# Two matrix products issued among the attention's last steps, and one PSUM pool for both stages

## The chip, the cores and the metric

The kernel runs on one core of one Trainium2 chip. The metric is the device time of one execution in microseconds (us); lower is better. The engines are named as the profile names them: PE (TensorE, matmuls; PEld is its weight load), DVE (VectorE), ACT (ScalarE), POOL (GpSimd), SP (SyncE, which issues the DMAs here). Each engine runs its own instructions in the order in which the program wrote them and waits on semaphores for the others.

## The reference

```python
def _attn_ref(q, k, v, w1, b1, w2):              # q, k, v: 4 x 8 heads x 576 x 64
    scores = scale * np.matmul(q, k.transpose(0, 1, 3, 2))
    x = (psi_rel / psi_i)[..., None]             # log1p of distances over log1p of the row
    bias = np.maximum(x @ w1 + b1, 0.0) @ w2     # one bias per head
    scores = scores + bias.transpose(2, 0, 1)[None]
    attn = softmax(scores)
    return np.matmul(attn, v)

def _moe_ref(x, w1, w2, w3, w_out):              # x: 2304 x 512, w1..w3: 512 x 768
    h = np.maximum(np.maximum(x @ w1, x @ w2), x @ w3)
    return h @ w_out
```

The attention's output, heads side by side, is the x of the second part. Everything is fp32 at the boundary.

## The kernel before

**Three stages.** First the bias of the attention is built and parked in HBM. Then the attention runs in 72 steps (`NSTEP`), one per tile of query rows, and four more steps without new scores (`LAG` is 4). Last comes the matrix stage: x times the three weight matrices with a maximum, then times w_out. The program is written in its final order (`manual_schedule`): what stands earlier in the code is earlier on its engine.

**An attention step.** Step n computes scores on PE (`front`), adds the bias and takes the maximum on DVE (`shift`), exponentials on ACT, normalization on POOL (`norm`), and, four steps late, `flip`: PE transposes the attention rows into the PSUM tiles `tp` (two) and `lp`, and ACT and DVE copy them to the tile `et`. Then `products` takes a few pieces of attention times values from a queue; their sum lies in the PSUM tile `pv`, which `split_x` (L427, DVE) copies into the blocks of x. In steps 72 to 75 no scores are made: each is a flip (transposes of 64 rows at a time, L366) and two or three pieces of `pv` (128 rows by 64 columns, L407). The last sum, `pvlast`, lies in a place of the tag `t`. Its last four matmuls read the tile `vl1`, the left-over rows of the values.

**The matrix stage** multiplies 2 x 2 block matrices by a scheme of seven products p1 to p7 instead of eight. x has the blocks b11, b12, b21, b22 and sums of them, t1 to t4; the weights too. Each operand is split into a high and a low part in a format that PE multiplies in one pass: `high` is a cast on ACT (L583), `low` a subtraction on DVE or POOL (L560, the line of the helper `arith`). A product is 2 x 3 matmuls (L670 high by high, L671 with the low part of x, L672 with the low part of the weights), six in all, of 128x128 by 384 columns. A group is the seven products of one third x of the tokens with one weight set s; the first groups are (s, x) = (0, 0), (1, 0), (0, 1), (1, 1). The order on PE is p5, p6, p2, p7, p1 of the next group, p4, p3.

**Three PSUM places per group.** p1, p5 and p2 each take a new place from `bank`. p6, p7 and p4 are added onto p1's place, p3 onto p5's. So each of them can start only when the one before it has been read out: p6 after ACT copied p1 (m1, L691), p7 after ACT copied p6 (u2, L699), p4 after ACT copied p7 (u3, L706), and p3 after DVE added u3 to p5 (in the first group the DVE instruction `ht<-p,u` whose inputs are p5 and u3; "p5's add" below).

**Work between the products.** Ahead of each product there is a slot in which listed jobs run (`at(n, k, ...)`: group n, slot k). Slot (0, 0) stands ahead of p5 of the first group. The jobs prepare the second third of x (`b1`) and weight set 1: `raise_w(1, 0)` and `raise_w(1, 1)` are its casts on ACT (768 and 1024 columns, into the tile `wh1`), `lower_w` the subtractions on DVE (`wl`).

**The end of the attention.** After step 75 the rest of `pv` and `pvlast` is issued, then t2's low part and the sum t4 on DVE, the cast of t4 on ACT, its low part on DVE, and `split_x` for `pvlast`. Only then is the attention's PSUM pool released and a new one opened with eight places of one tag, `p`.

**Places in SBUF.** The pools of the matrix stage have `reuse_waits="tile"`: the first instruction that writes a new tile waits for every user of each earlier tile that lies on any of the new one's bytes. In the program's address map of one partition, `wh1` lies at bytes 128160 to 135328. The attention's `bias3` (125344 to 129952), `bias4` (129952 to 134560), `vl0` (134560 to 135072) and `vl1` (135072 to 135584) lay there before. The tile of m1 (126624 to 128160) lies on `bias3` alone.

Lines that the text names beside these: L311 `shift`, L339 POOL's normalization, L477 and L481 the copies of the transposes, L747 and L749 `raise_w`.

Of the kernel before, what the change touches and what calls it, by code (L numbers as in the profile page):

```python
# [9 lines left out]
F32 = mybir.dt.float32  # L10
# [4 lines left out]
PSUM = bass.MemoryType.PSUM  # L15
# [4 lines left out]
def kernel(  # L20
# [12 lines left out]
    nc = tc.nc  # L33
# [13 lines left out]
    psums = []  # L47
    dram = ctx.enter_context(tc.tile_pool(name="dram", bufs=1, space=DRAM))

    def ps_s(name, tag="s"):  # L50
        return psums[-1].tile([128, 2, 512], F32, tag=tag, bufs=2, name=name)

    def early(name):
        return psums[-1].tile([128, 1024], F32, tag="bp", bufs=4, name=name)

    def bank(name):
        return psums[-1].tile([128, 512], F32, tag="p", bufs=8, name=name)

    def ps_t(name):
        return psums[-1].tile([128, 512], F32, tag="t", bufs=2, name=name)  # L60
# [3 lines left out]
    TW = 384  # L64
# [5 lines left out]
    xs = {}  # L70
# [142 lines left out]
    NSTEP = len(sched)  # L213
# [8 lines left out]
    class Attention:  # L222
# [125 lines left out]
        def flip(self, n):  # L348
            pair, y = fronts[n]
            which, t = step_of(pair, y)  # L350
            pool, e2 = self.pool, self.st.pop(n)["e"]
            if y == MIX:
                self.group(2 * pair + 1, 1)
                parts = [(2 * pair, GW, 0, LEFT), (2 * pair + 1, GW, LEFT, LEFT)]
            else:
                un = 2 * pair + which
                if y in (0, 2, 7):
                    self.group(un, int(y == 2))
                parts = [(un, 128 * (t % 2), 0, 128)]
            lp = psums[-1].tile([128, 128], F32, tag="l", bufs=1, name=f"lp{pair}_{y}")  # L360
            tps = [ps_t(f"tp{pair}_{y}_{r}") for r in range(2)]
            blocks = [(2 * c + h, S * h + 128 * c + LEFT * h) for h in range(2) for c in range(NTQ)]

            def turn(r, to, k0):
                p = slice(64 * r, 64 * r + 64)
                return nc.tensor.transpose(to, e2[p, k0:k0 + 128], ident[p, p])  # L366

            a = turn(0, lp[:, 0:64], LB)
            for i, (o, k0) in enumerate(blocks):
                turn(1, tps[1][:, 64 * o:64 * o + 64], k0)  # L370
                turn(0, tps[0][:, 64 * o:64 * o + 64], k0)
            b = nc.tensor.nop()
            tc.add_manual_dep(b.ins, a.ins.name, mybir.DependencyInfo(
                mybir.DependencyClass.Sync, mybir.DependencyReason.DATA), reason="two row tiles write one bank")
            turn(1, lp[:, 64:128], LB)
            out = []
            for r in range(2):
                src = tps[r].rearrange("p (c h q) -> p c h q", c=NTQ, h=2)
                un, c0 = parts[r if y == MIX else 0][0:2]
                c0 += 0 if y == MIX else 64 * r  # L380
                out.append([(self.et[un][0][:, :, :, c0:c0 + 64], src)])
            out.append([(self.et[un][1][:, c0:c0 + w], lp[:, r:r + w]) for un, c0, r, w in parts])
            return out

        def queue_pv(self, un, g, ea, el):
            hp, b = units[un]
            u = self.data[un]
            made = []
            x = GW if (hp + g) % 2 else 0
            ranges = [(x, GW)] + ([(2 * GW, LEFT)] if g else [])  # L390
            w0 = sum(w for _, w in ranges)
            last = un == len(units) - 1 and not g

            def pair(c):
                def run():
                    if c == 0:
                        self.split_x()

                        if last:
                            made.append(ps_t("pvlast")[:, 0:w0])  # L400
                        else:
                            made.append(psums[-1].tile([128, w0], F32, tag="pv", bufs=1, name=f"pv{un}_{g}"))
                    pv = made[0]
                    for h in range(2):
                        p = slice(64 * h, 64 * h + 64)
                        w, x = (u["vt"][:, c, h], ea[:, c, h]) if c < NTQ else (u["vl"][:, h], el)
                        nc.tensor.matmul(pv[p], lhsT=w, rhs=x, start=(c == 0), stop=(c == NTQ))  # L407
                    if c == NTQ:
                        slot = ((1, 0), (2, 3))[hp // 2][b // (B // 2)]
                        o = 0  # L410
                        for c0, w in ranges:
                            col = (b % (B // 2)) * S + c0
                            for x in range(NX):
                                lo, hi = max(col, TW * x), min(col + w, TW * x + TW)
                                if lo < hi:
                                    self.done.append((pv[:, o + lo - col:o + hi - col],
                                                      raws[x][slot][:, hp % 2, lo - TW * x:hi - TW * x]))
                            o += w
                        return True
                return run  # L420

            self.wait = True
            self.pvq.extend(pair(c) for c in range(NTQ + 1))
# [7 lines left out]
        def step(self, n, more=(), behind=()):  # L431
            m, f = n - BATCH, n - LAG
            if n < NSTEP:
                pair, y = fronts[n]
                which, t = step_of(pair, y)
                un = 2 * pair + which
# [29 lines left out]
            ends = bool(done) or n % NS == 7  # L466

            def empty():
                tp0, tp1, left = self.flip(f)
                if lead and n < NSTEP:  # L470
                    for h in range(2):
                        self.shift(n, h)
                    if split:
                        self.expo(n, 0)
                shared = FILL + 2 <= n < NS + 2
                for x in tp0 + ([] if shared else left):
                    nc.scalar.copy(*x)  # L477
                if turned:
                    products()
                for x in tp1 + (left if shared else []):  # L480
                    nc.vector.tensor_copy(*x)  # L481
# [45 lines left out]
            if n < NSTEP:  # L527
                pair, y = fronts[n]
                k = n - (NS * pair + (3 if pair else 5))
# [94 lines left out]
    wf = {}  # L624
# [21 lines left out]
    def sum_w(raw, sr):  # L646
        g = nc.gpsimd
        for o, a, b, op in ((part(sr, 0), part(raw, 0), part(raw, 2), ALU.add),
# [6 lines left out]
    PRODUCTS = dict(p1=(0, "b11"), p2=(2, "b21"), p3=(6, "b22"), p4=(1, "t4"), p5=(3, "t1"), p6=(4, "t2"),  # L655
                    p7=(5, "t3"))

    def moe(pool, wpool, x0, xa, xb, raw, sr):
        ht = pool.tile([128, NX, 4, TW], F32, name="ht", bufs=1)
        hd = h_d.rearrange("(f p) (t n) -> p f t n", p=128, t=2)  # L660
        xb_ = [x0] + [Blocks(x, xa, xb) for x in range(1, NX)]
        v, g = nc.vector, nc.gpsimd

        def terms(o, w, xn, r, first, last, again=False):
            hi, lo = w
            h, l = xn
            for j in range(2):
                c = slice(r + 128 * j, r + 128 * j + 128)
                on = dict(skip_group_check=again)
                nc.tensor.matmul(o, lhsT=hi[:, c], rhs=h[:, j], start=first and j == 0, stop=False, **on)  # L670
                nc.tensor.matmul(o, lhsT=hi[:, c], rhs=l[:, j], start=False, stop=False, **on)  # L671
                nc.tensor.matmul(o, lhsT=lo[:, c], rhs=h[:, j], start=False, stop=last and j == 1, **on)  # L672

        def group(s, x):

# [2 lines left out]
            o = {}  # L678
# [2 lines left out]
                return pool.tile([128, TW], F32, tag=name, bufs=bufs, name=f"{name}{s}_{x}")  # L681

            def made(p, on=None):
                o[p] = o[on] if on else bank(f"{p}_{s}_{x}")[:, 0:TW]
                w, n = PRODUCTS[p]
                terms(o[p], wf[s], xs[x][n], 256 * w, not on, True, bool(on))
                return o[p]
# [69 lines left out]
        b0, b1, b2 = xb_  # L757
        F = lambda f, *a: (lambda: f(*a))
        for k, what in {
                (0, 0): (F(b1.sum, "t1"), F(raise_w, 1, 0), F(b1.high, "b11"), F(lower_w, 1, 0, v, 3)),  # L760
                (0, 2): (F(raise_w, 1, 1),),
                (0, 3): (F(lower_w, 1, 3, v, 4),),
                (0, 4): (F(b1.high, "t1", "b21"),),
                (0, 5): (F(b1.low, "t1"), F(b1.sum, "t3")),
# [38 lines left out]
        for s in range(2, NSET):  # L803
            n = 3 * s - 3
# [70 lines left out]
        for x in range(len(order)):  # L875
            n = 4 + x
# [46 lines left out]
        n = 3 * NSET - 3  # L923
# [76 lines left out]
        n = 3 * NSET  # L1000
        for m in range(NP):
            at(*((n - 8, 0) if m == 0 else (n - 1, 0) if m == 1 else (n + m - 2, 0)), F(load_h, m))
            w = n + m - 1
# [109 lines left out]
    with tc.manual_schedule():  # L1113
# [3 lines left out]
        at = Attention(apool)  # L1117
        n = 0
# [198 lines left out]
            w.rest()  # L1317
        x0.low("t2")
        x0.sum("t4")
        x0.high("t4")  # L1320
        x0.low("t4")
        at.split_x()
        apool.release()
        psums.pop().release()
        psums.append(ctx.enter_context(tc.tile_pool(name="psum_m", bufs=1, space=PSUM, reuse_waits="tile")))
        xb = ctx.enter_context(tc.tile_pool(name="xb", bufs=1, side="right", reuse_waits="tile"))
        with tc.tile_pool(name="moe_p", bufs=1, reuse_waits="tile") as mp:
            moe(mp, wpool, x0, xa, xb, last["raw"], last["got"]["sr"])


_OUT = ((2304, 512), "float32")
# [43 lines left out]
```

## Time and profile before

| | before |
|---|---|
| median of 3 runs | 530.75 us (529.96 to 531.67) |
| the profiled execution | 530.31 us |
| its span in the profile | 528.4 us |
| PE busy | 518.6 us, 98% of the span |
| DVE, ACT, POOL busy | 437.5, 356.9, 261.4 us |
| attention's last flip / first matmul of the matrix stage | 257.20 / 261.30 us |

The profile is one execution. All its times count from the start of its span. The time outside the span is 1.9 us. A row of the timeline gives the start, the time taken, the engine, the line, the operation, what it writes and reads, and how many such instructions are merged; in brackets how long the engine was idle before and who released it. Matmuls overlap each other, so the distance from start to start tells the pace, not the time taken. The same holds in part for DVE and ACT, where one instruction begins about 0.1 us before the last has ended.

### The profile page before, as it was taken

The numbers are of one execution on the slowest core, as the hardware profiler recorded it, in microseconds if no ns is written. First come the engines' busy times: TensorE is split into PE (matmuls) and PEld (weight loads), VectorE is DVE, ScalarE is ACT, GpSimd is POOL, SyncE is SP. The second block draws the span as 40 slices with busy tenths as digits, with TensorE's granted clock in tenths as the row PEclk, the third lists the DMA queues.
The fourth block names the chain that finished last, engine by engine and source line by source line (L and its number), as shares of the span: only waits on it lengthen the run. The fifth ranks groups of instructions, "written<-read, shape, count | busy, mean of one in ns | idle before, by whom it ended". The sixth has DMA issues, their size and how long they took to land.

```text
span 528.4 us, 13630 instructions
## 1 busy us (share of the span) xinstructions
PE 518.6 (98%) x5167; PEld 433.5 (82%) x5167; DVE 437.5 (83%) x932; ACT 356.9 (68%) x802; POOL 261.4 (49%) x290
## 2 busy tenths in 40 slices
PE   8998999999999999999999999999999999999997
PEld 4464667676767676767699999999999999999997
DVE  7998979898989898988899888648887556898883
ACT  8997989999989999988666443442434425465552
POOL 0003877677878798887600055466637455300000
PEclk9999999999999999999999999999999999999999
DMA  5995988534675184214010115342247270856642
GB/s 161 277 334 164 326 280 224 178 96 122 198 244 153 25 235 126 71 24 143 3 40 2 40 56 188 137 145 95 78 167 253 81 243 7 258 166 194 187 154 81
DMA packets 73474, 78.66 MB, mean 149 GB/s; under 512 B 23168, under 2 KB 54528, under 8 KB 73408
## 3 DMA queue, kind: packets, MB, share of 16 engines
q1 hardware_dynamic: 73264, 77.49, 46.9%
q8 instruction: 41, 0.67, 0.5%
q10 hardware_dynamic: 144, 0.29, 0.2%
q14 instruction: 25, 0.20, 0.1%
HBM read 49.56 MB, written 27.94 MB: 147 GB/s over the span
## 4 chain that ended last, share of the span: by engine, by line
PE 95%; DVE 2%; issue 1%; DMA 1%; ACT 0%; DVEq 0%; ACTq 0%
PE pv L407 16%; PE p L670 13%; PE p L671 12%; PE p L672 12%; PE s L301 12%; PE bp L140 8%; PE tp L366 6%; PE p_o L1041 4%; PE p_o L1040 4%; PE p_o L1039 4%; PE s L291 2%; PE lp L366 2%; DVE sn L311 1%; DMA sm<-in_small_dram 1%; PE pvlast L407 0%
## 5 line engine op out<-in xcount | busy, mean ns | idle before, releaser
L339 POOL TENSOR_SCALAR e<-e,rc 128x576 f32<-128x576 f32 x144 | 111.2, 788 | 31.3 <-DVE rc L335 25.8
L311 DVE CUSTOM_DVE_ANT_0 sn<-s,bias 128x576 f32<-128x576 f32 x144 | 103.2, 754 | 23.2 <-PE lp L366 12.4
L325 ACT ACTIVATE e<-sn,nm 128x576 f32<-128x576 f32 x144 | 111.4, 780 | 5.6 <-DVE nm L311 5.4
L407 PE MATMUL pv<-et,vt 128*64 128x320 f32 (+1 forms) x496 | 74.0, 419 | 0.1
L366 PE MATMUL tp<-ident,e 64*128 64x64 f32 x1152 | 53.2, 224 | 0.5 <-ACT et L477 0.3
L481 DVE COPY et<-tp 128x512 f32<-128x512 f32 x72 | 49.3, 685 | 3.0 <-PE tp L366 2.9
L301 PE MATMUL s<-kh,qh 64*128 64x288 f32 x240 | 48.2, 343 | 2.8 <-DVE nm L311 2.7
L477 ACT COPY et<-tp 128x512 f32<-128x512 f32 x72 | 41.8, 580 | 12.7 <-PE lp L366 11.9
L366 PEld LDWEIGHTS tp<-ident,e 64*128 64x128 f32 x1152 | 47.4, 139 | 0.9 <-ACT et L477 0.4
L301 PEld LDWEIGHTS s<-kh,qh 64*128 64x128 f32 x240 | 28.1, 185 | 23.2 <-DVE nm L311 9.2
L560 POOL TENSOR_TENSOR ws<-wr 128x256 f32<-128x256 f32 x16 | 12.4, 773 | 69.0 <-ACT u L699 49.6
L407 PEld LDWEIGHTS pv<-et,vt 128*64 128x64 f32 x496 | 30.2, 136 | 17.8 <-issue 1.6
L140 PE MATMUL bp<-hid,w2s 128*32 128x79 f32 (+51 forms) x640 | 40.3, 391 | 1.1 <-DVE hid L117 0.8
L699 ACT COPY u<-p 128x384 f32<-128x384 f32 x27 | 13.0, 480 | 41.6 <-PE p L672 41.5
L301 PE MATMUL s<-kl,qh 64*128 64x288 f32 x240 | 41.0, 296 | 0.0
L301 PE MATMUL s<-kh,ql 64*128 64x288 f32 x240 | 39.9, 291 | 0.0
L117 DVE TENSOR_SCALAR hid<-wls,bp 128x528 f32<-128x528 f32 (+17 forms) x108 | 39.0, 446 | 0.0
L140 PEld LDWEIGHTS bp<-hid,w2s 128*32 128x32 f32 x640 | 21.3, 109 | 20.7 <-issue 13.5
L706 ACT COPY u<-p 128x384 f32<-128x384 f32 x27 | 12.9, 479 | 36.9 <-PE p L672 36.7
L366 PE MATMUL lp<-ident,e 64*128 64x64 f32 x144 | 33.1, 230 | 1.1 <-ACT et L477 0.4
L560 DVE TENSOR_TENSOR q<-p,u 128x384 f32<-128x384 f32 x36 | 20.0, 555 | 14.4 <-ACT u L706 12.0
L366 PEld LDWEIGHTS lp<-ident,e 64*128 64x128 f32 x144 | 19.8, 137 | 13.6 <-issue 8.1
(209 smaller groups left out, 1625.9 us busy)
## 6 DMA issues: line engine op xcount, KB each, us to landing
bias_d<-bs SPq DMA_DIRECT2D x36, 295.5 KB, 5.4
w<-in_moe_w_dram SPq DMA_DIRECT2D x36, 256.0 KB, 3.1
bias<-bias_d SPq DMA_DIRECT2D x15, 576.0 KB, 5.2
h_d<-ht SPq DMA_DIRECT2D x18, 384.0 KB, 3.2
hin<-h_d SPq DMA_DIRECT2D x16, 384.0 KB, 4.5
qr<-in_qd_dram SPq DMA_DIRECT2D x16, 288.0 KB, 4.7
kr<-in_kd_dram SPq DMA_DIRECT2D x16, 288.0 KB, 5.1
vt<-in_v_dram SPq DMA_DIRECT2D x32, 128.0 KB, 2.8
```

Of the source, the lines that this page charges most:

```text
L140: nc.tensor.matmul(bp[32 * c:32 * c + 32, o:o + w], lhsT=w2s, rhs=src, start=True, stop=True)
L301: nc.tensor.matmul(ss[h][:, x, 0:HALF], lhsT=u[q][p, 128 * t:128 * t + 128], rhs=u[k][p, cols], start=(j == 0), stop=(j == len(terms) - 1))
L311: nc.vector.tensor_tensor_reduce(out=sn.rearrange("p (a b) -> p a b", a=2), in0=st["s"][h][:, :, 0:HALF], in1=bt.rearrange("p (a b) -> p a ...
L325: nc.scalar.activation(st["e"][:, S * h:S * h + S], sn, ACTF.Exp, scale=-1.0, bias=nm, accum_out=self.sm[:, x:x + 1])
L339: nc.gpsimd.tensor_scalar(out=e, in0=e, scalar1=self.rc[:, x:x + 1], scalar2=1.0, op0=ALU.mult, op1=ALU.mult)
L366: return nc.tensor.transpose(to, e2[p, k0:k0 + 128], ident[p, p])
L407: nc.tensor.matmul(pv[p], lhsT=w, rhs=x, start=(c == 0), stop=(c == NTQ))
L477: nc.scalar.copy(*x)
L481: nc.vector.tensor_copy(*x)
L670: nc.tensor.matmul(o, lhsT=hi[:, c], rhs=h[:, j], start=first and j == 0, stop=False, **on)
L671: nc.tensor.matmul(o, lhsT=hi[:, c], rhs=l[:, j], start=False, stop=False, **on)
L672: nc.tensor.matmul(o, lhsT=lo[:, c], rhs=h[:, j], start=False, stop=last and j == 1, **on)
```

## The change

The matrix stage takes its PSUM places from the attention's tags instead of a pool of its own: six in turn, two of tag `s`, two of `t`, one `l`, one `pv`. The attention's pool therefore stays open to the end. p1 and p5 of group (0, 0) are issued inside the attention: p1 in step 73 ahead of the flip, p5 in step 74 behind the flip. `terms` moves out of `moe` for that. The group later takes them from `ahead`. The cast and the low part of t4 and the `split_x` of `pvlast` move from the end of the attention into slot (0, 0), behind both casts of weight set 1 on ACT and behind its first subtraction on DVE; `raise_w(1, 1)` moves there from slot (0, 2), and t1 and b11 of the second third stand behind them.

```diff
+    ring = []
+
     def bank(name):
-        return psums[-1].tile([128, 512], F32, tag="p", bufs=8, name=name)
+        if not ring:
+            ring.extend("ssttlp")
+        k = ring.pop(0)
+        if k == "s":
+            return ps_s(name)[:, 0]
+        return ps_t(name) if k == "t" else one_bank(name, "l" if k == "l" else "pv")
+
+    def one_bank(name, tag):
+        return psums[-1].tile([128, 512], F32, tag=tag, bufs=1, name=name)
...
             def empty():
+                if n == NSTEP + 1:
+                    begin("p1")
                 tp0, tp1, left = self.flip(f)
+                if n == NSTEP + 2:
+                    begin("p5")
...
-    def moe(pool, wpool, x0, xa, xb, raw, sr):
+    def terms(o, w, xn, r, first, last, again=False):
...
+    ahead = {}
+
+    def begin(p):
+        w, n = PRODUCTS[p]
+        ahead[p] = bank(f"{p}_0_0")[:, 0:TW]
+        terms(ahead[p], wf[0], xs[0][n], 256 * w, True, True)
+
+    def moe(pool, wpool, x0, xa, xb, raw, sr, split_x):
...
             def made(p, on=None):
+                if (s, x) == (0, 0) and p in ahead:
+                    o[p] = ahead[p]
+                    return o[p]
...
-                (0, 0): (F(b1.sum, "t1"), F(raise_w, 1, 0), F(b1.high, "b11"), F(lower_w, 1, 0, v, 3)),
-                (0, 2): (F(raise_w, 1, 1),),
+                (0, 0): (F(raise_w, 1, 0), F(raise_w, 1, 1), F(b0.high, "t4"), F(lower_w, 1, 0, v, 3), F(b0.low, "t4"),
+                         split_x, F(b1.sum, "t1"), F(b1.high, "b11")),
                 (0, 3): (F(lower_w, 1, 3, v, 4),),
...
         x0.low("t2")
         x0.sum("t4")
-        x0.high("t4")
-        x0.low("t4")
-        at.split_x()
         apool.release()
-        psums.pop().release()
-        psums.append(ctx.enter_context(tc.tile_pool(name="psum_m", bufs=1, space=PSUM, reuse_waits="tile")))
```

The tiles `lp` and `pv` are also taken as whole places of 512 columns (`one_bank`) and cut to size.

## Rows read from the trace of the kernel before

**Rows 1.** The page: busy time, share of the span and instructions of each engine.
```profile
PE 518.6 (98%) x5167; PEld 433.5 (82%) x5167; DVE 437.5 (83%) x932; ACT 356.9 (68%) x802; POOL 261.4 (49%) x290
```

**Rows 2.** Chain that ended last, around the last attention sum: start, us, what.
```profile
259.20 2.17 PE pvlast L407 x20
```

**Rows 3.** Stretches: busy time and instructions of each engine, PE clock, DMA share, GB/s.
```profile
249.00:252.00 3.00, 2.40 (x30) 1.37 (x28) 2.58 (x7) 2.97 (x10) 2.00 (x4) 1.00 0.61 224
...
268.70:276.00 7.30, 7.30 (x44) 7.30 (x44) 7.27 (x11) 4.46 (x9) 0.00 (x0) 1.00 0.21 68
276.00:283.30 7.30, 7.30 (x43) 7.14 (x41) 7.27 (x11) 4.27 (x7) 0.00 (x0) 1.00 0.00 0
```

**Rows 4.** Timeline of PE, 253 to 264 us.
```profile
253.22 0.22 PE L366 MATMUL lp<-ident,e 64*128 64x64 f32 x1
253.37 0.76 PE L407 MATMUL pv<-et,vt 128*64 128x320 f32 x4
...
255.15 0.22 PE L366 MATMUL lp<-ident,e 64*128 64x64 f32 x1
255.44 1.84 PE L407 MATMUL pv<-et,vt 128*64 128x320 f32 x12
...
259.04 1.90 PE L407 MATMUL pvlast<-et,vt 128*64 128x256 f32 x16
260.76 0.61 PE L407 MATMUL pvlast<-et,vl 128*64 128x256 f32 x4
261.30 0.44 PE L670 MATMUL p<-b11h,wh 128*128 128x384 f32 x1
261.58 0.34 PE L671 MATMUL p<-b11l,wh 128*128 128x384 f32 x1
...
263.49 0.33 PE L670 MATMUL p<-t2h,wh 128*128 128x384 f32 x1
```

**Rows 5.** The low weights: the last instruction before 261 us that writes them.
```profile
L560 DVE TENSOR_TENSOR wl<-ws,wh x1: 967/967/967, 239.1 to 239.1; 128x512 fp32r<-128x512 f32 x1
```

**Rows 6.** Timeline of DVE, 259 to 283 us.
```profile
259.82 0.95 DVE L560 TENSOR_TENSOR t2l<-t,t2h 128x768 fp32r<-128x768 f32 x1
260.68 0.95 DVE L560 TENSOR_TENSOR t<-xb,t 128x768 f32<-128x768 f32 x1
262.66 0.96 DVE L560 TENSOR_TENSOR t4l<-t,t4h 128x768 fp32r<-128x768 f32 x1 [1.03 <-ACT t4h L583]
...
264.74 0.95 DVE L560 TENSOR_TENSOR wl<-wr,wh 128x768 fp32r<-128x768 f32 x1
265.77 0.56 DVE L560 TENSOR_TENSOR ht<-p,m 128x384 f32<-128x384 f32 x1
...
267.38 0.55 DVE L560 TENSOR_TENSOR ht<-p,u 128x384 f32<-128x384 f32 x1
268.06 0.96 DVE L560 TENSOR_TENSOR t1l<-t,t1h 128x768 fp32r<-128x768 f32 x1
...
282.80 0.55 DVE L560 TENSOR_TENSOR ht<-p,u 128x384 f32<-128x384 f32 x1
```

**Rows 7.** Timeline of ACT, 261 to 266 us.
```profile
261.72 0.83 ACT L583 CAST t4h<-t 128x768 fp32r<-128x768 f32 x1 [2.96 <-DVE t L560]
...
263.02 0.84 ACT L747 CAST wh<-wr 128x768 fp32r<-128x768 f32 x1
263.76 0.84 ACT L583 CAST b11h<-xb 128x768 fp32r<-128x768 f32 x1
264.73 0.48 ACT L699 COPY u<-p 128x384 f32<-128x384 f32 x1
265.11 1.05 ACT L749 CAST wh<-ws 128x1024 fp32r<-128x1024 f32 x1
```

**Rows 8.** Timeline of PE at p3 of the third group.
```profile
283.13 0.34 PE L672 MATMUL p<-t4h,wl 128*128 128x384 f32 x1
283.40 0.45 PE L670 MATMUL p<-b22h,wh 128*128 128x384 f32 x1
```

More of the change, by code (lines that the diff above doesn't have):

```diff
@@ L359, in flip @@
                 parts = [(un, 128 * (t % 2), 0, 128)]
-            lp = psums[-1].tile([128, 128], F32, tag="l", bufs=1, name=f"lp{pair}_{y}")
+            lp = one_bank(f"lp{pair}_{y}", "l")[:, 0:128]
             tps = [ps_t(f"tp{pair}_{y}_{r}") for r in range(2)]
@@ L401, in run @@
                         else:
-                            made.append(psums[-1].tile([128, w0], F32, tag="pv", bufs=1, name=f"pv{un}_{g}"))
+                            made.append(one_bank(f"pv{un}_{g}", "pv")[:, 0:w0])
                     pv = made[0]
@@ L656 @@
                     p7=(5, "t3"))
-    def moe(pool, wpool, x0, xa, xb, raw, sr):
+    def terms(o, w, xn, r, first, last, again=False):
+        hi, lo = w
+        h, l = xn
+        for j in range(2):
+            c = slice(r + 128 * j, r + 128 * j + 128)
+            on = dict(skip_group_check=again)
+            nc.tensor.matmul(o, lhsT=hi[:, c], rhs=h[:, j], start=first and j == 0, stop=False, **on)
+            nc.tensor.matmul(o, lhsT=hi[:, c], rhs=l[:, j], start=False, stop=False, **on)
+            nc.tensor.matmul(o, lhsT=lo[:, c], rhs=h[:, j], start=False, stop=last and j == 1, **on)
+    ahead = {}
[4 more added lines that the diff above has]
+    def moe(pool, wpool, x0, xa, xb, raw, sr, split_x):
         ht = pool.tile([128, NX, 4, TW], F32, name="ht", bufs=1)
@@ L662, in moe @@
         v, g = nc.vector, nc.gpsimd
[L664 to L672, printed above, removed]
         def group(s, x):
@@ L1319 @@
         x0.sum("t4")
-        x0.high("t4")
-        x0.low("t4")
-        at.split_x()
         apool.release()
-        psums.pop().release()
-        psums.append(ctx.enter_context(tc.tile_pool(name="psum_m", bufs=1, space=PSUM, reuse_waits="tile")))
         xb = ctx.enter_context(tc.tile_pool(name="xb", bufs=1, side="right", reuse_waits="tile"))
         with tc.tile_pool(name="moe_p", bufs=1, reuse_waits="tile") as mp:
-            moe(mp, wpool, x0, xa, xb, last["raw"], last["got"]["sr"])
+            moe(mp, wpool, x0, xa, xb, last["raw"], last["got"]["sr"], at.split_x)
+        psums.pop().release()
 _OUT = ((2304, 512), "float32")
```

## The prediction

> **What bounds the kernel now.** I read the page's busy shares first: PE works 98% of the span [rows 1]. Then the chain that ended last: around the border of the two stages it runs on PE alone, through the pieces of `pv`, `pvlast` (2.17 us) and then the products without a break [rows 2]. Then the stretches: PE is full from 268.70 to 283.30 us, and DVE nearly so, 7.27 of 7.30 us twice [rows 3]. DVE therefore has no room to catch up there. The timeline shows that it already sets PE's start in one place: p3 of the third group begins 0.27 us after the matmul before it instead of the usual 0.17, and p5's add on DVE ended at 282.80 + 0.55 = 283.35, 0.05 us before p3's 283.40 [rows 6, 8]. So the kernel is bound by PE, and around the border by whatever makes PE late; work that only moves along PE gains nothing. The change can gain where PE waits now, and lose where ACT or DVE come later than PE needs them.
>
> **What PE gains and loses in the last steps.** I call the start of the first product 261.30 us S. p1 and p5 take S to 263.49, 2.19 us; 0.11 of it is the longer distance behind the first matmul (0.28 against 0.17), so the twelve matmuls are 2.08 [rows 4]. They don't vanish: they are issued earlier, and everything behind them in steps 73 to 75 moves back by the same 2.08.
>
> Each of the two adds one border between unlike shapes on PE. Such borders are in the rows: the last two pairs of `pvlast` take 0.54 to the first product, where pairs follow each other at 1.72 / 8 = 0.215, so 0.11 is lost, and another 0.11 behind the first matmul [rows 4]. No row has a product followed by a transpose or by `pv`. From below such a border costs 0, from above 0.22. p1 stands between `pv` and transposes, where there was a border already; its own start is the measured one, so I take 0.22 for it. p5 stands between transposes and `pv`; I take 0.11, the middle. p5 also fills a wait: in step 74 `pv` starts 0.29 us behind the last transpose, in step 73 0.15 [rows 4], so 0.14 goes. Together PE comes to the matrix stage 0.22 + 0.11 - 0.14 = 0.19, say 0.2 us later in net; the ends are -0.14 (borders free) and 0.44 (both dear, the wait not filled). PE's larger idle time, 0.6 of the 3 us from 249 to 252 [rows 3], lies in step 72, ahead of p1, and stays. The operands are there: the low weights were complete at 239.12 + 0.97 = 240.09 [rows 5].
>
> The Trainium skill, in "TensorEngine Tiling (Array Packing)", section Tiling Modes, says that a change of the tiling mode drains TensorE, which speaks against the change: both products stand between modes. By it both borders are dear and the term would be 0.22 + 0.22 - 0.14 = 0.30, and the sum below 0.1 more. The border that rows 4 show agrees with it; those that the change makes, no row shows.
>
> **What ACT does next.** p6 now is the first product behind `pvlast`; call its start P. It takes the place that p1 had, so P = S + 2.08 + 0.2 = 263.6. ACT has copied m1 long before, since p1 was done in step 73, and goes to the job list: both casts of weight set 1, then t4's cast, then b11's of the second third, then u2.
>
> The first of these casts now waits. It is the first write to `wh1`, which shares its last 256 bytes with `vl1`, and `vl1` is read by the last four matmuls of `pvlast` [rows 4]. A new tile's first write waits for all users of what lay on its bytes, so the cast starts when `pvlast` has ended, although it doesn't itself write those bytes. Before, this wait couldn't be seen: the cast stood behind m1 and began at 263.02, 1.72 us behind the first product [rows 7]. `pvlast`'s last matmul ends about when the first product starts, so I set the cast at P + 0.1.
>
> From there ACT works back to back, with distances from start to start of [rows 7]: 0.74 for a 768-wide cast (263.02 to 263.76), 0.95 for the 1024-wide one (1.05 less the usual overlap of 0.1). So: first cast P + 0.11, second P + 0.85, t4 P + 1.80, b11 P + 2.54, u2 P + 3.28, ended P + 3.76. p7 may start at P + 3.80. Undisturbed it would start two products and one border behind P, at P + 0.11 + 2 x 1.04 = P + 2.19. **PE stalls 1.61 us ahead of p7.** Before, u2 ended at 264.73 + 0.48 = 265.21 and p7 was due at 263.49 + 2 x 1.04 = 265.57: no stall, because the 1024-wide cast stood behind u2 and t4's ahead of the first product.
>
> If the wait on `vl1` weren't there, ACT would wait for t4's sum instead. That sum follows `pv`'s last copy and t2's low part on DVE, all behind PE, so it keeps its distance: 260.68 + 0.95 = S + 0.33, now P + 0.33. Then t4's cast starts at P + 0.42 and u2 ends at P + 2.38: a stall of 0.23. These are the two ends of this term; I take the upper, because the overlap of the bytes is a fact of the program.
>
> **What DVE does next.** Before, it idled 1.03 us ahead of t4's low part [rows 6]; the new order puts weight set 1 there. But t4's cast ends at P + 2.63, so the low part starts at P + 2.7. From that one's start to p5's add were 267.38 - 262.66 = 4.72 us, of which 265.77 - 264.74 = 1.03 were weight set 1's, now done ahead [rows 6]. So p5's add starts at P + 6.39 and ends at P + 6.94; p3 may start at P + 6.99. PE reaches p3 three products behind p7, at P + 6.92. So PE is late by 0.07 more here. The `split_x` for `pvlast` lies in this block at about P + 3.6 to P + 4.0; the next p1 takes `pvlast`'s place at P + 4.84, so it costs nothing.
>
> p3 was at 263.49 + 5 x 1.04 = 268.69 = S + 7.39. It is now at P + 6.99 = S + 9.27: 1.9 us late. DVE is later than that: its add was at S + 6.08 and is at S + 2.28 + 6.39 = S + 8.67, 2.6 late. It wins back the idle ahead of `t1l`, 268.06 against 267.93 and the overlap of 0.08, 0.21 in all, and then nothing to 282.80, where it is full [rows 3, 6]. So p3 of the third group, which follows p5's add by 0.05 already [rows 8], comes **2.38 us late**. Behind it PE is as busy as before and has no slack to give this back.
>
> **Parts at nothing.** Six places in turn instead of eight: p1's place is next written two groups on, five products (5.2 us) behind p4, p5's seven products behind p3, while p5's add, for example, ended at 267.93, 1.3 us after p7 [rows 6]. If readers came over 5 us late it would cost their excess. The attention's own readers of the places of `s` end before: the last scores are read in step 71, two steps ahead of p1. One pool less to open and release costs nothing, since no wait stood at 261.30 but the border. No DMA moves on SP's queue, and POOL has no new work; its last two low parts are needed by p2 and p3 only.
>
> **The sum.** 0.2 in the last steps, 1.61 + 0.07 at p7 and p3 of the first group, and 0.5 that DVE's lag adds by the third group: 2.4 us. The profiled execution (span 528.4, its own time 530.31) would take 532.7. The median of the runs is 0.44 above that execution; with it I predict 533.1.
>
> **Rivals.**
>
> First, ACT doesn't wait for `pvlast`. Then the stall at p7 is 0.23, p3 starts at P + 5.6 (three products behind P + 2.42, and p5's add ends at P + 1.34 + 3.69 + 0.55 = P + 5.58), DVE's add is 2.28 + 5.03 - 6.08 = 1.23 late, less 0.21 is 1.0. 530.75 + 1.0 = 531.8. For it: nothing in the trace shows the wait. Against it: the bytes.
>
> Second, on the other side: ACT and DVE keep up. DVE no longer idles its 1.03 us, and weight set 1 is prepared while PE is still at `pvlast`. It decides at whether both casts are done before t4's sum, at P + 0.33, that is, started by P - 1.4, and t4's sum comes that early too. Then p3's late start goes (0.10 in the third group [rows 8], as much again for the slow matmul behind it, and, as an estimate, the same in the fourth: 0.4), and the wait of 0.14: 530.75 - 0.5 = 530.2. For it: DVE's idle time is real, and ACT has nothing else to do ahead of P. Against it: t4's sum stands behind `pv`'s last copy, which stands behind the two moved products.
>
> Third, the change doesn't do what it says: a product waits in step 73 or 74 for its place or its operands, and the flip behind it waits too. Rows 5 speak against it; it would cost what it waits, and at some tenths be no different from the first rival, 531.5.
>
> **How the numbers follow.** The forecast has 0.62, with a range of its own from 532.5 to 533.7 (its unknown borders, -0.14 to 0.44, and the scatter of a median); the first rival 0.20, the second 0.13, the third 0.05. The range is 531.0 to 534.0: it takes in the first and the third rival and leaves out the second and the tails. About 0.3% is what a measurement of this kernel can tell from no change, 1.6 us, so the bounds are 529.2 and 532.3. Slower by more: nine tenths of the forecast and a little of the first rival, 0.60. Within: the rest of these, the third rival and most of the second, 0.33. Faster: 0.07.
>
> **What would show it.** In the changed kernel's timeline: six products' matmuls ahead of the transposes of step 73 and six behind those of step 74, with `pv` 0.15 to 0.4 us behind; `wh` on ACT starting within 0.2 us of `pvlast`'s end, and ACT idle ahead of it; u2 about 3.3 us behind p6's start; a gap of 1.6 us on PE ahead of p7, put down to ACT; DVE's idle ahead of t4's low part moved to the cast of t4; no further wait on PE except short ones at p3. The prediction is wrong if `wh` starts before `pvlast` ends, if PE's sum of gaps from 249 to 291 us grows by less than a microsecond, or if PE later wins the time back.

## The result, and the profile after

The changed kernel takes 532.55 us (median of five runs, 532.34 to 535.16); the kernel before took 529.96 in the same comparison (five runs, 529.63 to 531.67). The ratio is 1.0057, 95% interval 1.0037 to 1.0077: slower by about 3 us. The profiled execution took 532.68 us with a span of 530.8, against 530.31 and 528.4.

The page of the changed kernel, its line of busy times, which answers to [rows 1]: as many instructions on each engine, PE 2.9 us longer busy.

```profile
PE 521.5 (98%) x5167; PEld 434.2 (82%) x5167; DVE 436.5 (82%) x932; ACT 357.3 (67%) x802; POOL 261.0 (49%) x290
```

The chain that ended last, of the changed kernel, from `pvlast` on (start, us, what), answers to [rows 2]. It no longer stays on PE: behind `pvlast` it goes through five operations of ACT and comes back at p7.

```profile
260.69 2.18 PE pvlast L417 x20
262.89 0.27 ACT wh L771
263.17 0.47 issue
263.63 0.52 ACT wh L773
264.23 0.36 issue
264.58 0.83 ACT t4h L597
265.41 0.73 ACT b11h L597
266.15 0.38 ACT u L723
266.53 0.04 issue
266.57 0.44 PE p L678
```

The waits of PE in the changed kernel (engine, line, what it waited for: total us, times, longest) have one entry that no wait of before answers to:

```profile
PE p L678 <- ACT u L723: 1.4, 1, 1.4
```

The timeline of PE in the changed kernel (start, time taken, instruction, how often; in brackets the idle time and its releaser), in the stretch of [rows 4], shifted by the two products:

```profile
251.77 0.44 PE L678 MATMUL p<-b11h,wh 128*128 128x384 f32 x1
...
252.75 0.34 PE L680 MATMUL p<-b11h,wl 128*128 128x384 f32 x1
253.02 0.27 PE L376 MATMUL lp<-ident,e 64*128 64x64 f32 x1
...
255.50 0.22 PE L376 MATMUL lp<-ident,e 64*128 64x64 f32 x1
255.65 0.45 PE L678 MATMUL p<-t1h,wh 128*128 128x384 f32 x1
255.93 0.34 PE L679 MATMUL p<-t1l,wh 128*128 128x384 f32 x1
...
256.65 0.34 PE L680 MATMUL p<-t1h,wl 128*128 128x384 f32 x1
256.92 1.84 PE L417 MATMUL pv<-et,vt 128*64 128x320 f32 x12
...
262.78 0.44 PE L678 MATMUL p<-t2h,wh 128*128 128x384 f32 x1
...
264.79 0.34 PE L680 MATMUL p<-b21h,wl 128*128 128x384 f32 x1
266.57 0.44 PE L678 MATMUL p<-t3h,wh 128*128 128x384 f32 x1 [1.44 <-ACT u L723]
...
284.99 0.44 PE L678 MATMUL p<-b22h,wh 128*128 128x384 f32 x1
```

p1 and p5 stand where the change puts them, and p6 of the first group (262.78) comes straight behind `pvlast`. Between p2's last matmul (264.79) and p7's first (266.57) lie 1.78 us instead of 0.17.

ACT of the changed kernel, 262 to 267 us, answers to [rows 7]. It waits for `pvlast`, and then works back to back until u2.

```profile
262.89 0.83 ACT L771 CAST wh<-wr 128x768 fp32r<-128x768 f32 x1 [2.26 <-PE pvlast L417]
263.63 1.05 ACT L773 CAST wh<-ws 128x1024 fp32r<-128x1024 f32 x1
264.58 0.83 ACT L597 CAST t4h<-t 128x768 fp32r<-128x768 f32 x1
265.32 0.83 ACT L597 CAST b11h<-xb 128x768 fp32r<-128x768 f32 x1
266.05 0.47 ACT L723 COPY u<-p 128x384 f32<-128x384 f32 x1
```

DVE of the changed kernel, 262 to 285 us, answers to [rows 6]; the last row is p5's add of the third group, which ends 0.05 us ahead of p3:

```profile
262.17 0.95 DVE L574 TENSOR_TENSOR t<-xb,t 128x768 f32<-128x768 f32 x1
263.76 0.96 DVE L574 TENSOR_TENSOR wl<-wr,wh 128x768 fp32r<-128x768 f32 x1 [0.64 <-ACT wh L771]
265.52 0.96 DVE L574 TENSOR_TENSOR t4l<-t,t4h 128x768 fp32r<-128x768 f32 x1 [0.80 <-ACT t4h L597]
...
269.19 0.55 DVE L574 TENSOR_TENSOR ht<-p,u 128x384 f32<-128x384 f32 x1
...
284.39 0.55 DVE L574 TENSOR_TENSOR ht<-p,u 128x384 f32<-128x384 f32 x1
```

**Two stretches make up the difference.** I measure the border from the start of step 71's `pv` group with the left-over values (248.72 before, 247.83 after; "the anchor" below), ahead of everything that the change moves, to the start of p3 of the third group. Before that was 283.40 - 248.72 = 34.68 us, after 284.99 - 247.83 = 37.16: 2.48 longer. From there to the output stage both profiles agree to 0.01 us, so nothing is given back. The second stretch I had not looked for: the output stage, from its first to its last matmul, took 68.18 before and 68.97 after, 0.79 more. The rest of the difference of the two spans, -0.89, lies ahead of the border (the anchor itself moves by that much), and a second profile of each kernel shows that this part is chance (below). 2.48 + 0.79 = 3.27 us lies inside the interval of the ratio, 2.0 to 4.1 us.

### The profile page after: what moved, and what is told of

It reads as the page before. It is cut to its first block, busy times and chain, and to the rows that moved or that the text cites. A ratio compares the mean times of both kernels' runs of the same rounds, so it can differ in the third digit from the quotient of the medians.

```text
span 530.8 us, 13631 instructions
## 1 busy us (share of the span) xinstructions
PE 521.5 (98%) x5167; PEld 434.2 (82%) x5167; DVE 436.5 (82%) x932; ACT 357.3 (67%) x802; POOL 261.0 (49%) x290
## 4 chain that ended last, share of the span: by engine, by line
PE 95%; DVE 2%; issue 1%; ACT 1%; DMA 1%; DVEq 0%; ACTq 0%
PE pv L417 16%; PE p L678 13%; PE p L680 12%; PE p L679 12%; PE s L311 12%; PE bp L150 7%; PE tp L376 6%; PE p_o L1065 4%; PE p_o L1064 4%; PE p_o L1063 4%; PE lp L376 2%; PE s L301 2%; DVE sn L321 1%; DMA sm<-in_small_dram 1%; ACT e L335 0%
```

## The experiments

The theory: ACT's first cast of weight set 1 waits for `pvlast` only because `wh1` shares 256 bytes with `vl1`; the casts queued behind it hold u2, and PE stands 1.6 us at p7; DVE, late as well and full, carries the rest on. The rivals: the ring of six places costs something by itself; the two products cost PE more than 0.2; or ACT would be late without the shared bytes too.

The border stretch of every run, its difference and the output stage's to the kernel before, and what the timed runs say (ratio less one, times the median of before in the same comparison, with its interval), in us:

```
run                  border  differs  output  sum   timed [95%]
before               34.68
after                37.16   +2.48    +0.79   3.3   3.0 [2.0, 4.1]
e1_vl_first          35.80   +1.12    +0.79   1.9   1.8 [1.2, 2.4]
e2_old_order         36.66   +1.98    +0.78   2.8   2.6 [2.0, 3.2]
e3_products_back     36.41   +1.73    +0.78   2.5   1.9 [1.2, 2.6]
e4_ring_alone        34.68    0.00    +0.53   0.5   0.5 [-0.4, 1.4]
e5_t4_early          35.95   +1.27    +0.79   2.1   2.2 [1.5, 2.8]
e6_p1_in_72          36.33   +1.65    +0.79   2.4   2.8 [2.2, 3.4]
e7_before_t4_early   38.05   +3.37    +0.78   4.2   5.3 [4.4, 6.2]
e8_u2_first          36.28   +1.60    +0.54   2.1   2.4 [1.7, 3.1]
e9_b22_late          35.03   +0.35    +0.54   0.9   1.3 [0.5, 2.0]
e10_p1_in_72         34.78   +0.10    +0.80   0.9   0.9 [0.2, 1.6]
e11 (before again)   34.68    0.00    -0.01
e12 (after again)    37.16    0.00 *  -0.01 *          * to after
```

In the expectations of the first eight the stretch is mostly counted from the flip of step 72, 1.08 us later: 33.60 before, 36.08 after. No expectation ahead of e11 held the output stage's share, so most timed differences stand above those expected (1.8 for 1.0 in e1, 2.6 for 2.0 in e2, 2.4 for 1.5 in e8). In e7 alone the sum lies outside the timed interval; in five of its six timed executions the granted clock was 0.994 to 0.997, in the profiled one 1.00.

**e1: the shared bytes taken away.** The tiles of `vl` are placed ahead of the bias tiles, so `wh1` no longer lies on `vl1`; no instruction changes its place on its engine.

```diff
-            bias_t.extend(pool.tile([128, 2, S], F32, ...
             self.vl = [pool.tile([128, 2, D], F32, ...
+            bias_t.extend(pool.tile([128, 2, S], F32, ...
```

> The changed kernel with the tiles vl0 and vl1 ahead of the bias tiles, so that wh1 no longer lies on vl1; nothing else differs. I measure the stretch from the first transpose of step 72 to p3 of the third group: 33.60 us before, 36.08 in the changed kernel. Theory (the first cast of weight set 1 waits for pvlast, and u2 stands behind it): the cast starts right behind m1, over 2 us before pvlast ends; the gap ahead of p7 falls from 1.78 to 0.4 (a stall of 0.23 that t4's late sum leaves), the stretch to 34.6, and the time to about 1.0 us over the kernel before. Rivals (the six places in turn, or the moved products themselves, make PE late): the stretch stays at 36.1 and the time at 2.4 us over.

ACT of this kernel, in the place of the rows of after; p6 starts at 262.53 here:

```profile
260.26 0.85 ACT L771 CAST wh<-wr 128x768 fp32r<-128x768 f32 x1
261.00 1.07 ACT L773 CAST wh<-ws 128x1024 fp32r<-128x1024 f32 x1
262.96 0.84 ACT L597 CAST t4h<-t 128x768 fp32r<-128x768 f32 x1 [0.90 <-DVE t L574]
263.70 0.83 ACT L597 CAST b11h<-xb 128x768 fp32r<-128x768 f32 x1
264.44 0.47 ACT L723 COPY u<-p 128x384 f32<-128x384 f32 x1
```

The cast starts 2.27 us ahead of p6 instead of 0.11 behind it; ACT then waits for t4's sum, as the first rival said. The distance ahead of p7 falls from 1.78 to 0.41 us and the border by 1.36. The wait came from the shared bytes: shown. 1.12 us stay, so t4's late preparation and DVE cost as well.

**e2 and e3: one half of the change each.** e2 keeps the two products in the attention and takes back the order of the jobs; e3 keeps the new order and takes back the products.

```diff
e2:
-                (0, 0): (F(raise_w, 1, 0), F(raise_w, 1, 1), F(b0.high, "t4"), ...
+                (0, 0): (F(b1.sum, "t1"), F(raise_w, 1, 0), F(b1.high, "b11"), F(lower_w, 1, 0, v, 3)),
+                (0, 2): (F(raise_w, 1, 1),),
...
         x0.sum("t4")
+        x0.high("t4")
+        x0.low("t4")
+        at.split_x()
e3:
-                if n == NSTEP + 1:
-                    begin("p1")
-                if n == NSTEP + 2:
-                    begin("p5")
```

> The changed kernel with the old order of the jobs: t4's cast, its low part and the split of pvlast ahead of the matrix stage, the 1024-wide cast back in slot (0, 2). The two products stay among the attention's steps. Theory: moving the products takes away the time in which ACT and DVE prepared t4 and weight set 1, whatever the order; ACT does t4, m1, the 768-wide cast, b11 and then u2, which ends 3.5 us behind p6's start: a gap of 1.5 us ahead of p7, the stretch 35.6, the time 2.0 us over the kernel before. Rival (the new order alone makes it late): no gap ahead of p7, the stretch 33.8, the time 0.2 us over.

> The changed kernel with p1 and p5 issued where they were before, behind pvlast; the new order of the jobs and the six places stay. Theory: both casts, t4's and b11's stand ahead of u2 here too, behind m1: u2 ends 5.35 us behind p1's start, p7 was due at 4.27, so PE stalls 1.1 us there, DVE is 1.7 us late at the third group, the stretch is 35.3 and the time 1.7 us over the kernel before. Rival (the moved products alone make it late): the stretch 33.6, the time as before.

Both borders came out as expected, 35.58 and 35.33 from the flip. But e2's stall is at p6, not at p7: m1 stands behind t4's cast, which waits for t4's sum, so p6 waits for m1. The waits of PE in e2 and in e3:

```profile
PE p L678 <- ACT m L715: 1.6, 1, 1.6
```

```profile
PE p L674 <- ACT u L719: 1.0, 1, 1.0
```

Each half alone costs 1.7 to 2.0 us. In e3 p1 and p5 stand between `pvlast` and p6 as before, and ACT's longer queue ahead of u2 is enough to stop p7.

**e4: the ring alone.** Both edits together, so that of the change only the six places and the single pool are left.

> The kernel before with the one part of the change that is about PSUM: six places in turn from the attention's pool, which stays open; products and jobs where they were. Theory: no reader comes near to the 5 us that a place stays free, so the stretch is 33.6 and the time the same as before within 0.3 us. Rival (the six places make PE wait): gaps at p1, p5 or p2 and some of the 2.5 us that the stretch has grown by.

The border is the one of before to the hundredth and the time the same (1.001, 0.9992 to 1.0027). Six places for eight cost nothing there.

**e5 to e7: prepare t4 earlier.** e5 is e1 with t2's low part and t4's sum on DVE in step 74, behind t3's low part, and with t4's cast and low part ahead of the jobs of slot (0, 0); e6 puts p1 into step 72 besides, where PE waits; e7 moves the same two DVE operations in the kernel before.

```diff
             x0.low("t3")
+            x0.low("t2")
+            x0.sum("t4")
             yield "scalar"
             x0.high("b22")
...
-        x0.low("t2")
-        x0.sum("t4")
+        x0.high("t4")
+        x0.low("t4")
e6, besides:
-                if n == NSTEP + 1:
+                if n == NSTEP:
                     begin("p1")
```

> The kernel of e1_vl_first with t2's low part and the sum t4 on DVE in step 74, behind t3's low part, and t4's cast and low part ahead of the job list of slot (0, 0). DVE was idle for 2.1 us ahead of the last copy of transposes in the changed kernel, so these 1.8 us should fit there. Theory (PE was late since ACT and DVE prepared t4 and weight set 1 too late): no gap ahead of p6 or p7, p3 of the third group no longer behind DVE; the stretch from the first transpose of step 72 to p3 of the third group 33.7 (33.60 before, 36.08 in the changed kernel, 34.72 in e1), the time that of the kernel before within 0.4 us. Rival (the moved products cost PE in themselves): 34.5 or more, 1 us over.

> The kernel of e5 with p1 one step earlier, in step 72 ahead of the flip, where PE waits 0.6 us in all for copies of the step before. From the pv matmuls ahead of that flip to p3 of the third group it was 34.68 us before and 37.16 in the changed kernel. Theory: p1 fills the wait, 0.6 less than e5: 34.2, and a time 0.5 us under the kernel before, if DVE and ACT keep up. Rival (the copies are late because ACT and DVE are, and the flip only waits behind p1 instead): 34.8, the time as in e5.

> The kernel before with t2's low part and the sum t4 in step 74, the products where they were. Theory (the moved products make the room on DVE that e5 uses; without them there is none): t3's low part ends there at 258.25 and the last copy of transposes follows at 258.17, so the two instructions push that copy back by 1.8 us, and pvlast with it: the stretch 35.2, the time 1.6 us over the kernel before. Rival (t4 early is good by itself): the stretch 33.4, the time 0.2 under.

All three missed. In e5 the stall at p7 is gone, but there is a new one of 0.8 us ahead of `pvlast`, for DVE's copy of the last transposes. DVE of e5, with the sum that holds the copy up, and POOL of e5 beside it:

```profile
257.40 0.94 DVE L574 TENSOR_TENSOR t2l<-t,t2h 128x768 fp32r<-128x768 f32 x1
258.27 2.57 DVE L574 TENSOR_TENSOR t<-xb,t 128x768 f32<-128x768 f32 x1
260.76 0.68 DVE L495 COPY et<-tp 128x512 f32<-128x512 f32 x1
```

```profile
257.45 2.57 POOL L574 TENSOR_TENSOR b22l<-xb,b22h 128x768 fp32r<-128x768 f32 x1 [0.79 <-ACT b22h L597]
```

The sum takes 0.95 us elsewhere and 2.57 here; POOL's subtraction ends at 260.02 and the sum 0.82 later, about its usual length. In e6 and e7 t3's low part (2.29 and 2.28) and t2's (2.57 twice) are hit, and `pvlast` waits 2.0 and 3.1 us. e7 also shows that the rearrangement is no gain without the change.

**e8: u2 first.** In the changed kernel `raise_w(1, 1)` and the cast of b11 go behind u2.

```diff
-                (0, 0): (F(raise_w, 1, 0), F(raise_w, 1, 1), F(b0.high, "t4"), ...
+                (0, 0): (F(raise_w, 1, 0), F(b0.high, "t4"), F(lower_w, 1, 0, v, 3), F(b0.low, "t4"),
+                         split_x, F(b1.sum, "t1")),
+                (0, 2): (F(raise_w, 1, 1), F(b1.high, "b11")),
```

> The changed kernel with its old places in SBUF, but with the 1024-wide cast and b11's cast behind u2, in slot (0, 2). Theory: the first cast still waits for pvlast, but u2 ends 2.1 us behind p6's start and p7 no longer waits for it (2.19). DVE is the next in line: the second subtraction of weight set 1 waits for the 1024-wide cast, p5's add ends 6.1 us behind p6's start, p3 is due at 5.3 and waits 0.8; the stretch is 35.1 and the time 1.5 us over the kernel before. Rival (p7's wait was all of it): 33.9 and 0.3 over.

PE of e8 at p3 of the first group:

```profile
268.49 0.45 PE L678 MATMUL p<-b22h,wh 128*128 128x384 f32 x1 [0.52 <-DVE ht L574]
```

The stall at p7 is gone (no distance over 0.2 us), and p3 comes 0.86 us behind the matmul ahead of it instead, waiting for DVE. Of the 1.61 us only 0.88 (36.08 to 35.20) is won: DVE is next in line.

**e9 and e10: the same, with POOL out of the way.** e9 is e5 with b22's low part on DVE behind the loop; e10 puts p1 into step 72 besides.

```diff
             x0.high("b22")
-            yield "vector"
-            x0.low("b22", nc.gpsimd)
...
+        x0.low("b22")
         x0.high("t4")
         x0.low("t4")
```

> The changed kernel with the tiles of vl placed apart and t4's sum prepared in step 74, as in e5, but b22's low part taken from POOL and given to DVE behind the loop, so that POOL computes nothing beside t4's sum. From the start of the last group of pv with the low values (step 71) to p3 of the third group: 34.68 us before, 37.16 with the change, 35.80 in e1, 35.95 in e5. Theory (ACT and DVE come late, PE itself loses only the 0.2 us of the borders; e5 missed because POOL's low part stretched t4's sum from 0.95 to 2.57 us): t4's sum takes 0.95, p6 starts 14.95 behind that anchor, no gap over 0.2 at p7 or p3, 34.8 in all, the time 0.1 over before, ratio 0.999 to 1.002. Rival (DVE has no room for the two operations in step 74 whatever POOL does): t4's sum 0.95, but pvlast waits for DVE's copy again, 35.5 or more, the time 0.8 over before or more.

> e9 with p1 a step earlier, in step 72, where PE waits 0.6 us. From the same anchor to p3 of the third group: if DVE keeps up, 34.8 less 0.7 = 34.1, 0.5 us below the kernel before. But without p1 in step 73 DVE's t3 low meets POOL's b21 low again (2.29 us in e6, 1.04 in e5), and the copy ahead of pvlast comes behind it: e6's 36.33 less the 1.6 that POOL's second low part cost = 34.7, the time as before, ratio 0.999 to 1.001. I expect the latter.

DVE of e9 and, below it, DVE of e10 in step 74:

```profile
256.05 1.03 DVE L574 TENSOR_TENSOR t3l<-t,t3h 128x768 fp32r<-128x768 f32 x1
257.01 0.95 DVE L574 TENSOR_TENSOR t2l<-t,t2h 128x768 fp32r<-128x768 f32 x1
257.88 0.94 DVE L574 TENSOR_TENSOR t<-xb,t 128x768 f32<-128x768 f32 x1
```

```profile
255.14 2.29 DVE L574 TENSOR_TENSOR t3l<-t,t3h 128x768 fp32r<-128x768 f32 x1
257.35 0.95 DVE L574 TENSOR_TENSOR t2l<-t,t2h 128x768 fp32r<-128x768 f32 x1
258.22 0.95 DVE L574 TENSOR_TENSOR t<-xb,t 128x768 f32<-128x768 f32 x1
```

In e9 t4's sum takes 0.94, no wait of PE is left at `pvlast`, p6 or p7, and the border is 35.03, 0.35 above the kernel before. I expected 34.8. From the anchor to p6 are 14.95, as expected, 0.18 more than before; the slow first matmul of p6 behind `pvlast` (0.11) I had left out, and p3 of the third group waits about 0.07 longer than before. The rival, that DVE has no room in step 74, falls. In e10 t3's low part is stretched as expected, `pvlast` waits 0.4 us for DVE, and the border is 34.78 (expected 34.7). In e9, with ACT and DVE early enough, the two moved products so cost 0.35 us; in e10, where p1 also fills PE's wait of step 72, 0.10. They gain nothing. Both kernels are still timed 0.2% slower (1.0024, interval 1.001 to 1.0038; 1.0017, 1.0003 to 1.003), more than I expected: in e10's profile nearly all of that is the output stage (0.80 of 0.9), in e9's 0.54 of 0.9. Neither beats the kernel before, and no other version did.

**e11 and e12: both kernels once more**, each in one more execution.

> The kernel before, unchanged, profiled once more. From the anchor to p3 of the third group 34.68, as in its first profile, if the order of the work sets this stretch and not chance. The output stage from its first to its last matmul was 68.18 in that profile and 68.71 to 68.97 in the nine others: 68.18 again if the kernel's own order sets it, up to 68.97 if it differs from one execution to the next.

> The changed kernel, unchanged, profiled once more. From the anchor to p3 of the third group 37.16 again, with 1.78 us between the matmuls ahead of p7; the output stage 68.97 again, or less if chance sets it.

The borders repeat, 34.68 and 37.16, and so do the output stages, 68.17 and 68.96. What doesn't repeat lies ahead of the border: the anchor is at 247.61 in the second profile of before, 248.72 in the first. So the output stage's difference belongs to the programs. PE in the output stage from 500 to 512 us (busy us and matmuls, clock, DMA share, GB/s), first the kernel before, then its second profile, then the changed kernel:

```profile
500.00:512.00 12.00, 12.00 (x108) 1.00 0.60 178
```

```profile
500.00:512.00 12.00, 12.00 (x108) 1.00 0.57 176
```

```profile
500.00:512.00 12.00, 12.00 (x104) 1.00 0.63 190
```

At the same granted clock, 1.00, PE does 108 matmuls where the changed kernel does 104. Start to start they stand 0.113 us apart in both profiles of before from the 308th to the 505th of the stage, and elsewhere mostly 0.118, as in the changed kernel throughout. In e4, e8 and e9, whose output stage is 68.7, the pace goes over to 0.113 a few matmuls behind the 505th, where the stream has a short break, and stays there to the end. Why is open: no experiment was aimed at it. The new ring of places is not needed for the longer stage (e7 has the old pool and 68.96), nor is another order of PE's instructions, since e7's edit moves only work of DVE.

## Why the prediction was right

The forecast, 533.1 us, named the right side and mechanism. Its terms, one by one:

- **PE's borders: 0.2 us.** Measured 0.17: from the first transpose of step 72 to p6, 13.69 before and 13.86 after. p1's first matmul has the long distance (0.28), its last stands 0.27 ahead of the transposes, `pv` 0.27 behind p5's last matmul (0.17 within a product), and p5 comes 0.15 behind the last transpose, as the filled wait required. By the rule of the Trainium skill's "TensorEngine Tiling (Array Packing)", Tiling Modes, priced in the prediction from rows 4, the term was 0.30; the trace gives less, though the borders at products' ends show 0.10 each.
- **The cast at P + 0.11, u2's start at P + 3.28, p7 at P + 3.80.** Measured 262.89, 266.05 and 266.57 with P = 262.78, that is P + 0.11, P + 3.27 and P + 3.79. The stall is 1.78 - 0.17 = 1.61, as forecast. That the wait is caused by bytes which the cast doesn't write was argued from the address map and is now shown by e1.
- **p5's add at P + 6.39, p3 at P + 6.99.** Measured P + 6.41 and P + 7.03. The 0.07 at p3 came out, but not for the reason given: p3 starts 0.17 behind the matmul ahead of it (269.64 to 269.81), so PE did not wait for the add; the slow first matmul of the stalled p7 (0.28 instead of 0.17), which the prediction's "three products" left out, made PE that late by itself.
- **p3 of the third group 2.38 us late.** Measured 2.48: DVE, full between the two, gave back nothing beyond its idle.
- **The first rival, without the wait,** was priced at 1.0 us; e1, which takes the wait away, has 1.12 in the border.
- **Six places at nothing.** e4 shows it for the border.
- **The second rival, that ACT and DVE keep up,** would have gained 0.5 us. In e9 t4's cast and both casts of weight set 1 are done at P + 0.26 (261.71 + 1.07, with P = 262.52) and PE waits for neither engine at p6 and p7, and still its border is 0.35 longer than before. The rival was priced too well: p3 of the third group stands 0.35 behind the matmul ahead of it in e9, against 0.27 before, so that wait is not gone, and PE pays its borders anyway. The test isn't clean there, since e9 also gives DVE b22's low part.

Two sizes that the sum didn't hold cancelled in the median. The median of before was 530.75 when I wrote and 529.96 in the comparison, 0.79 lower. And the output stage is 0.79 us longer, which nothing in the prediction allows for. The measured median is 0.55 below the forecast even so, within the spread of either kernel's runs. So the right total owes something to chance; the border's 2.4 against 2.48 owes none but the 0.07 above.

## What to carry to other kernels

Work that moves earlier on one engine uncovers what stood behind it on the others: before pricing it, list the queue of each helper engine up to the first result that the bound engine needs next, and ask of each new first entry what it waits for, places in memory shared with older tiles included. Where a pool waits for whole tiles, as here, a tile that shares a few bytes with one still in use waits for all its users, and e1 took 1.36 us off the border by exchanging two lines. And where tenths of a per cent count, compare the stages far from the change as well: here about a quarter of the loss in the profiles arose some 190 us behind it.

## What the runs showed of the hardware that I had not expected

- A subtraction or sum on DVE with both inputs in SBUF takes 0.95 us alone, and 2.28 to 2.57 when a POOL subtraction of the same shape runs beside it; in e5 POOL's too took 2.57 instead of 1.81, having started 0.05 us behind a DVE operation. The Trainium skill, in "SBUF — State Buffer", section Who interferes with whom, says that a DVE instruction with two SBUF inputs contends with a GpSimd instruction that reads SBUF. The same section of the Trainium skill says that issue order, not the shape of the operation, decides who blocks. The rows agree: in e5 each time the later starter is the longer one. Before the change t3's low part already paid this (2.28 us at 255.97, beside POOL's work), and in the changed kernel p1 in step 73 moves the two nearly apart (1.06).
- The same program repeats such a long stretch to 0.01 us (34.68 twice, 37.16 twice), while its start in the span moved by 1.1 us between two executions.
- The output stage's matmuls run at one of two paces, 0.113 or 0.118 us, at one granted clock. Where a program changes from one to the other repeats in a second profile (before: from the 308th to the 505th, twice); nothing tried here explains it.
